# Eight banks of maxima on VectorE alone, and another order of steps, in a two-stream attention kernel

## The chip, the cores and the metric

The kernel runs on one core of one Trainium2 chip. The metric is the device time of one execution in microseconds; the number given for a kernel is the median of its runs.

## The reference

Two attention blocks A and B with the same input x (2048 tokens, 512 channels, 32 heads of 16) and weights of their own are mixed by a gate for each token. All arithmetic is in float32.

```python
def attention(x, wqkv, wo):                 # both blocks
    q, k, v = split(x @ wqkv)               # 32 heads of 16
    scores = einsum("bhqd,bhkd->bhqk", q, k) * 16 ** -0.5
    p = softmax(scores, axis=-1)
    o = einsum("bhqk,bhkd->bhqd", p, v)
    return merge_heads(o) @ wo

g = sigmoid((x * gate_w).sum(-1, keepdims=True))
out = g * attention(x, A_wqkv, A_wo) + (1 - g) * attention(x, B_wqkv, B_wo)
```

## The kernel before

The 64 heads of both blocks are worked through one after the other. A stage ahead of the main loop projects q, k and v, writes them to DRAM in high and low parts, and computes the maxima of the first head and of four more rounds. Then the main loop goes over `ROUNDS` = 64 x 16 *rounds*, two at a time; two rounds are called a *pair* here, and eight pairs make a head.

A round has three sorts of work.

- **Scores** (`score`, L594, letter `e`): the scores are computed transposed, keys on partitions. A round takes 128 keys and all 2048 queries: four products of 512 columns (L602), each into one of the three banks of `ps_st`, and ScalarE's exponential reads each (L604) into a quarter of `p`. `p` has three buffers, one per round. The row maximum is not subtracted by an engine: its two parts stand as two more rows in `q_st` (rows 48 and 49 of a half of 64 rows), against rows of -1 in `k_st`.
- **Maxima** (`max_product`, L116, letters `m`, `A`, `B`, `x`): the maxima are computed 20 rounds ahead of the scores that need them (`m = r + NT + LEAD`), with queries on partitions. A round takes 128 queries and all 2048 keys: four products of 512 columns (L128). The first two go into single banks (`ps_m1`, two buffers that alternate), the third and fourth (`A`, `B`) into the two banks of `ps_m2`, which has one buffer. VectorE reads a single bank, or both banks of `ps_m2` at once after `B`, and leaves a maximum for each query in `mxp` (L139).
- **V products** (`attend`, L555, digits): a round of `p` against V, for four stretches of keys in four column groups of TensorE (L563), accumulated over the 16 rounds of a head in the one bank `acc`. A digit says how many quarters of 128 queries follow; 4 is a whole round, 2 is half of one. Each `attend` writes eight matmul records into the trace. After the last round of a head ScalarE evicts `acc` (L580), and the next head's first V product waits for that.

Scores and maxima use 50 and 48 rows of TensorE's 128, so that two products, one on rows from 0 and one on rows from 64, run side by side; `rows()` alternates the halves, and each digit sets it back to 0.

The order of all of this is written out by hand as one string for a pair, and is the order in each engine's queue:

```python
    FULL = "eem4emeAeB2emex2AyeB"
    LATE = "ee2ee2ee2ee2"
```

`LATE` serves the last pairs, which have no maxima left to compute. With `x`, one single bank of the pair takes a detour (except in the one pair of a head whose second round is the head's last, `mm % NT == NT - 1`): ScalarE copies the bank to SBUF (L133), GpSimd takes the larger of the two halves in three steps (L134 to L136), and `y`, in the next pair, lets VectorE read the 256 maxima that remain (L147).

At special places of a head more is queued. At the end of the pair that completes a head's maxima VectorE makes `mrow` from `mxp` (L157) and GpSimd splits it (L158, L159). In the pair after, at a digit that comes after the third `e`, `max_rows` lets VectorE transpose it (`mt`, L164), and SP sends it out and back into `q_st` (L167, L169). Functions in `later` run ahead of a pair's first step: loads, the reciprocals of the denominators (`invert_den`, L400, twice after every eighth head), and others. Output projections (`project_out`, L436) run ahead of a pair's first digit; eight of the 64 heads have them, one in each of four pairs.

Of the kernel before, what the change touches and what calls it, by code (L numbers as in the profile page):

```python
# [23 lines left out]
F32 = mybir.dt.float32  # L24
# [3 lines left out]
ALU = mybir.AluOpType  # L28
AX = mybir.AxisListType
# [3 lines left out]
P = 128  # L33
# [4 lines left out]
NT = S // P  # L38
# [13 lines left out]
def gated_mha(ctx: ExitStack, tc: tile.TileContext, xT, x, wqkv_a, wo_a, wqkv_b, wo_b, gate_w, out):  # L52
    nc = tc.nc
    pe, act, dve, pool = nc.tensor, nc.scalar, nc.vector, nc.gpsimd
# [4 lines left out]
    small = ctx.enter_context(tc.tile_pool(name="small", bufs=2))  # L59
# [26 lines left out]
    def load_stacks(h, halves=HALVES):  # L86
        dma = nc.sync.dma_start
        s, hh = divmod(h, H)
        g, j = divmod(hh, HG)
        q, k = q_st[h % 3], k_st[h % 3]  # L90
        qs, ks = qd[s][g], kd[s][g]

        def pairs(t, step):
            v = t[0, j]
            return bass.AP(tensor=v.tensor, offset=v.offset, ap=[[S, DH], [step, 2], [1, S]])

        for b in halves:
            dma(k[b:b + 32].bitcast(F32), pairs(ks, HG * DH * S))
            dma(q[b:b + 32].bitcast(F32), pairs(qs, 0))
            dma(k[b + 32:b + 48].bitcast(F32), ks[0, j])  # L100
            dma(q[b + 32:b + 48].bitcast(F32), qs[1, j])
# [5 lines left out]
    PARTS = ((0,), (1,), (2, 3))  # L107
    mxp = {}
    turn = [0]
    banks_m, halved = {}, []  # L110

    def rows():
        turn[0] ^= 1
        return HALVES[1 - turn[0]]

    def max_product(m, c, fold=False):  # L116
        h, t = divmod(m, NT)
        if t == 0 and c == 0:
            mxp[h] = small.tile([P, NT, 3], F32, name="mxp")
        q, k = q_st[h % 3], k_st[h % 3]  # L120
        part = min(c, 2)
        if c < 3:
            n = len(PARTS[part])
            banks_m[m] = (ps_m1 if n == 1 else ps_m2).tile([P, n * 512], F32, name=f"ps_m{n}")
        ps = banks_m[m]
        b = rows()
        o = max(0, c - 2) * 512
        pe.matmul(ps[:, o:o + 512], q[b:b + SC, t * P:(t + 1) * P], k[b:b + SC, c * 512:(c + 1) * 512],  # L128
                  start=True, stop=True)
        if fold:  # L130
            x = small.tile([P, 512], F32, name="fold", bufs=2)
            d = x[:, :256]
            act.copy(x, ps)  # L133
            pool.tensor_tensor(d, d, x[:, 256:], op=ALU.subtract)  # L134
            pool.tensor_scalar(d, d, 3.4028234e38, 0.0, op0=ALU.min, op1=ALU.max)  # L135
            pool.tensor_tensor(d, d, x[:, 256:], op=ALU.add)  # L136
            halved.append((mxp[h][:, t, part:part + 1], d))
        elif c != 2:
            dve.tensor_reduce(mxp[h][:, t, part:part + 1], ps, op=ALU.max, axis=AX.X)  # L139

    def max_part(m, part):
        for c in PARTS[part]:
            max_product(m, c)

    def max_halved():
        o, d = halved.pop(0)
        dve.tensor_reduce(o, d, op=ALU.max, axis=AX.X)  # L147

    mparts = {}

    def max_split(h):
        halves = mxp.pop(h)
        m = small.tile([P, NT], F32, name="mrow")
        mp = small.tile([P, 2, NT], F32R, name="mparts")
        dve.tensor_reduce(m, halves, op=ALU.max, axis=AX.X)  # L157
        pool.tensor_copy(mp[:, 0], m)  # L158
        pool.tensor_tensor(mp[:, 1], m, mp[:, 0].bitcast(F32), op=ALU.subtract)  # L159
        mparts[h] = mp  # L160

    def max_rows(h):
        mt = small.tile([P, 32], F32, name="mt")
        dve.transpose(mt, mparts.pop(h).rearrange("p i t -> p (i t)").bitcast(F32))  # L164
        q = q_st[h % 3]
        r = md[h % 3]
        nc.sync.dma_start(r.rearrange("i (t a x) -> a (i t) x", a=4, x=32), mt)  # L167
        for b in HALVES:
            nc.sync.dma_start(q[b + SC:b + SC + 2].bitcast(F32), r)  # L169
# [266 lines left out]
    def project_out(side, t):  # L436
        groups = SIDES[side]
        ps = result_bank()
        c, tt = divmod(t, 4)
        sl = slice(tt * P, (tt + 1) * P)  # L440
        for G in groups:
            n, g = gh[G] * DH, G % NG
            slot = c if G == LAST else g
            for i, (a, b) in enumerate(((0, 0), (1, 0), (0, 1))):
                pe.matmul(ps, ot[a][:n, slot, sl], wt[b][:n, g], start=G == groups[0] and i == 0,  # L445
                          stop=G == groups[-1] and i == 2)
        g = gate[min(side, 1)][:, t:t + 1]
        if side == 0:
            dve.tensor_scalar(o_acc[:, t], ps, g, None, op0=ALU.mult)
        else:  # L450
            dve.scalar_tensor_tensor(o_acc[:, t], ps, g, o_acc[:, t], op0=ALU.mult, op1=ALU.add)
# [134 lines left out]
    def attend_next(n):  # L586
        while n:
            r, qa = divmod(done[0], 4)
            qb = min(4, qa + n)
            attend(r, qa, qb)  # L590
            done[0] += qb - qa
            n -= qb - qa

    def score(r, c):  # L594
        h, kt = divmod(r, NT)
        if c == 0:
            pt[r] = ppool.tile([P, S], F32, name="p")
        q, k = q_st[h % 3], k_st[h % 3]
        kk, cc = (4 * (kt % 4) + c, kt // 4) if h == NH - 1 else (kt, c)
        b = rows()  # L600
        ps = ps_st.tile([P, 512], F32, name="ps_st")
        pe.matmul(ps, k[b:b + SC + 2, kk * P:(kk + 1) * P], q[b:b + SC + 2, cc * 512:(cc + 1) * 512],  # L602
                  start=True, stop=True)
        act.activation(pt[r][:, c * 512:(c + 1) * 512], ps, AF.Exp, scale=SCALE)  # L604
# [1 line left out]

    FULL = "eem4emeAeB2emex2AyeB"
    LATE = "ee2ee2ee2ee2"  # L610
    after = {}

    for r in range(0, ROUNDS, 2):
        h, kt = divmod(r, NT)
        projects = []
        for rr in (r, r + 1):
            for fn, a in later.pop(rr, ()):
                if fn is project_out:
                    projects.append(a)
                else:  # L620
                    fn(*a)
        if kt == 0 and h + 2 < NH:
            load_stacks(h + 2)
        m = r + NT + LEAD
        scored = parts = 0
        waiting = len(halved)
        for step in FULL if m < ROUNDS else LATE:
            if step == "e":
                score(r + scored // 4, scored % 4)
                scored += 1  # L630
            elif step in "mABx":
                mm, c = m + parts // 4, parts % 4
                max_product(mm, c, step == "x" and mm % NT != NT - 1)
                parts += 1
            elif step == "y":
                if waiting:
                    max_halved()
            else:
                for a in projects:
                    project_out(*a)  # L640
                projects = []
                turn[0] = 0
                if r:
                    attend_next(int(step))
                if scored > 2 and r in after:
                    max_rows(after.pop(r))
        m += 1
        if m < ROUNDS and m % NT == NT - 1:
            max_split(m // NT)
            after[r + 2] = m // NT  # L650
# [29 lines left out]
```

## Time and profile before

| | |
|---|---|
| runs | 2844.14, 2844.75, 2844.58 us; median 2844.58 |
| profiled execution | span 2843.0 us; its own time outside the span is not listed, the runs' median is 1.6 us longer |
| TensorE clock granted | 0.998 |
| busy, of the span | TensorE 98%, VectorE 87%, ScalarE 85%, GpSimd 37% |
| chain that ended last | TensorE 74%, VectorE 16%, ScalarE 8%, issue 2% |
| main loop | from about 300 us to the end |

In rows of the profile PE is TensorE, PEld its weight loads, DVE VectorE, ACT ScalarE, POOL GpSimd, SP the engine that issues DMAs. A row of the timeline gives the start in us, the duration in us, engine, line, operation, output and inputs, and how many like instructions in a row are merged (x5); shapes are those of the first of them, and a bracket tells how long the engine had stood idle and who ended that. Records of one engine overlap a little, so that the distance from one start to the next is shorter than a duration. A row of busy times by stretch gives the stretch, its length, and for each engine busy us and instructions, then clock, DMA share and GB/s. A row of groups gives count, busy us, mean ns of one, idle time before and who ended it. A row of waits gives the total us, the number of waits and the longest.

### The profile page before, as it was taken

What the parts mean: (1) busy time and instruction counts of PE and PEld (TensorE: products, weight loads), DVE (VectorE), ACT (ScalarE), POOL (GpSimd) and SP (SyncE); (2) the same over time, 40 slices, a digit from 0 to 9 for tenths busy, and PEclk for the clock granted to TensorE, in tenths of its full rate; (3) what the DMA queues carried; (4) which work ended last, traced back from release to release, by engine and by line L of the source; (5) the groups of instructions that cost most, each with busy time, mean ns of one, the idle gap of its engine ahead of it and who ended that gap; (6) DMA issues with size and microseconds to landing.
All of it is one profiled execution on the core that took longest, in us unless ns stands there. A gap on an engine that the chain in (4) does not pass through costs nothing.

```text
span 2843.0 us, 56787 instructions
## 1 busy us (share of the span) xinstructions
PE 2795.6 (98%) x22168; PEld 1230.1 (43%) x22168; DVE 2464.7 (87%) x3367; ACT 2412.5 (85%) x4696; POOL 1042.4 (37%) x1686
## 2 busy tenths in 40 slices
PE   8999999999999999999999999999999999999999
PEld 6877433333333333333333444433333333334445
DVE  3135899999999999999999988899999999998884
ACT  3221799999999999999999877899999999998785
POOL 1000355453433333333433555333333344345431
PEclk9999999999999999999999999999999999999999
DMA  6673333222332222232432342232222233233302
GB/s 237 203 229 122 82 69 78 58 52 54 66 58 55 55 43 58 52 56 54 85 54 52 92 94 62 54 56 51 60 43 56 54 70 70 54 72 80 76 6 91
DMA packets 83747, 214.30 MB, mean 75 GB/s; under 512 B 21878, under 2 KB 32086, under 8 KB 70934
## 3 DMA queue, kind: packets, MB, share of 16 engines
q1 hardware_dynamic: 80918, 201.76, 31.2%
q0 software_dynamic: 2560, 8.91, 1.3%
q8 instruction: 174, 2.85, 0.4%
q14 instruction: 95, 0.78, 0.1%
HBM read 145.87 MB, written 64.74 MB: 74 GB/s over the span
## 4 chain that ended last, share of the span: by engine, by line
PE 74%; DVE 16%; ACT 8%; issue 2%; DMA 0%; SPq 0%; ACTq 0%
PE acc L563 28%; PE ps_st L602 22%; DVE mxp L139 14%; PE ps_m L128 12%; PE ps_pro L228 6%; ACT p L604 5%; PE ps_m L445 3%; PE ps_pro L251 3%; ACT ev L580 1%; ACT fold L133 1%; DVE mxp L147 1%; DMA raw<-in_xT 0%; DVE mrow L157 0%; PE ps_st L445 0%; DVE rn L400 0%
## 5 line engine op out<-in xcount | busy, mean ns | idle before, releaser
L139 DVE TENSOR_REDUCE mxp<-ps_m 128x1 f32<-128x512 f32 (+1 forms) x2633 | 2190.3, 890 | 135.1 <-PE ps_m L128 61.0
L604 ACT ACTIVATE p<-ps_st 128x512 f32<-128x512 f32 x4096 | 2153.5, 610 | 177.0 <-PE ps_m L128 100.5
L128 PE MATMUL ps_m<-k_st,q_st 48*128 48x512 f32 x4096 | 1407.2, 441 | 5.3 <-DVE mxp L139 0.8
L602 PE MATMUL ps_st<-q_st,k_st 50*128 50x512 f32 x4096 | 1379.8, 438 | 0.0
L563 PE MATMUL acc<-p,vg 128*17 128x256 f32 (+1 forms) x12360 | 1182.8, 455 | 29.5 <-ACT ev L580 28.0
L602 PEld LDWEIGHTS ps_st<-q_st,k_st 50*128 50x128 f32 x4096 | 662.1, 184 | 801.6 <-ACT p L604 748.0
L128 PEld LDWEIGHTS ps_m<-k_st,q_st 48*128 48x128 f32 x4096 | 677.1, 184 | 251.8 <-DVE mxp L139 233.0
L134 POOL TENSOR_TENSOR fold<-fold 128x256 f32<-128x256 f32 x439 | 321.1, 731 | 1096.5 <-ACT fold L133 1096.5
L563 PEld LDWEIGHTS acc<-p,vg 128*17 128x17 f32 x12360 | 205.3, 95 | 466.3 <-issue 414.6
L136 POOL TENSOR_TENSOR fold<-fold 128x256 f32<-128x256 f32 x439 | 322.1, 734 | 36.6
L133 ACT COPY fold<-ps_m 128x512 f32<-128x512 f32 x439 | 261.3, 595 | 0.0
L135 POOL TENSOR_SCALAR fold<-fold 128x256 f32<-128x256 f32 x439 | 175.6, 400 | 38.5
L147 DVE TENSOR_REDUCE mxp<-fold 128x1 f32<-128x256 f32 x439 | 179.5, 409 | 0.0
L158 POOL CAST mparts<-mrow 128x16 fp32r<-128x16 f32 x64 | 12.6, 197 | 401.0 <-DVE mrow L157 401.0
L232 ACT CAST part<-ps_pro 128x1024 fp32r<-128x1024 f32 x32 | 32.5, 1015 | 132.9 <-PE ps_pro L228 132.9
L233 DVE TENSOR_TENSOR part<-ps_pro,part 128x1024 fp32r<-128x1024 f32 x32 | 39.2, 1225 | 111.4 <-ACT part L232 111.4
L445 PE MATMUL ps_m<-wo,ot 128*128 128x512 f32 (+1 forms) x354 | 90.9, 401 | 0.0
L254 ACT COPY v_st<-ps_pro 128x512 f32<-128x512 f32 x31 | 18.2, 587 | 77.4 <-PE ps_pro L251 77.4
L228 PE MATMUL ps_pro<-xh,whi 128*128 128x512 f32 x256 | 73.0, 404 | 8.8 <-ACT xh L214 8.7
L180 POOL DMA_DIRECT2D vg<-vd x32 | 25.6, 799 | 137.5 <-DMA vd<-v_st 137.1
L445 PEld LDWEIGHTS ps_m<-wo,ot 128*128 128x128 f32 (+1 forms) x354 | 63.9, 188 | 21.3 <-ACT fold L133 7.0
L228 PE MATMUL ps_pro<-xh,wlo 128*128 128x512 f32 x256 | 69.7, 395 | 0.0
(94 smaller groups left out, 822.1 us busy)
## 6 DMA issues: line engine op xcount, KB each, us to landing
k_st<-kd SPq DMA_DIRECT2D x128, 256.0 KB
q_st<-qd SPq DMA_DIRECT2D x128, 256.0 KB
qd<-part SPq DMA_DIRECT2D x32, 512.0 KB
kd<-part SPq DMA_DIRECT2D x32, 512.0 KB
k_st<-kd SPq DMA_DIRECT2D x128, 128.0 KB
q_st<-qd SPq DMA_DIRECT2D x128, 128.0 KB
od<-ev SPq DMA_DIRECT2D x63, 256.0 KB
vd<-v_st SPq DMA_DIRECT2D x32, 272.0 KB
```

Of the source, the lines that this page charges most:

```text
L128: pe.matmul(ps[:, o:o + 512], q[b:b + SC, t * P:(t + 1) * P], k[b:b + SC, c * 512:(c + 1) * 512], start=True, stop=True)
L133: act.copy(x, ps)
L134: pool.tensor_tensor(d, d, x[:, 256:], op=ALU.subtract)
L135: pool.tensor_scalar(d, d, 3.4028234e38, 0.0, op0=ALU.min, op1=ALU.max)
L136: pool.tensor_tensor(d, d, x[:, 256:], op=ALU.add)
L139: dve.tensor_reduce(mxp[h][:, t, part:part + 1], ps, op=ALU.max, axis=AX.X)
L147: dve.tensor_reduce(o, d, op=ALU.max, axis=AX.X)
L228: pe.matmul(ps[:, c * 512:(c + 1) * 512], a[:, k], b[:, k], start=n == 0, stop=n == 3 * KC - 1)
L445: pe.matmul(ps, ot[a][:n, slot, sl], wt[b][:n, g], start=G == groups[0] and i == 0, stop=G == groups[-1] and i == 2)
L563: pe.matmul(acc[32 * c:32 * c + 17, qa * P:qb * P], v[:, 4 * a + c if final else kt, j], p[:, c * 512 + qa * P:c * 512 + qb * P], start=fi ...
L602: pe.matmul(ps, k[b:b + SC + 2, kk * P:(kk + 1) * P], q[b:b + SC + 2, cc * 512:(cc + 1) * 512], start=True, stop=True)
L604: act.activation(pt[r][:, c * 512:(c + 1) * 512], ps, AF.Exp, scale=SCALE)
```

## The change

`FULL` becomes `"e2emem2ABmeee4emeAB"`. The letters `x` and `y` go, and with them ScalarE's copy, GpSimd's three steps and VectorE's read of the halved tile: the sixth product of a pair becomes an ordinary `m`, whose bank VectorE reads whole. The V products come in bursts of 2, 2 and 4 in place of 4, 2 and 2. `LATE`, the stage ahead of the loop and everything else stay.

```diff
-    banks_m, halved = {}, []
+    banks_m = {}
...
-    def max_product(m, c, fold=False):
+    def max_product(m, c):
...
-        if fold:
-            x = small.tile([P, 512], F32, name="fold", bufs=2)
-            d = x[:, :256]
-            act.copy(x, ps)
-            pool.tensor_tensor(d, d, x[:, 256:], op=ALU.subtract)
-            pool.tensor_scalar(d, d, 3.4028234e38, 0.0, op0=ALU.min, op1=ALU.max)
-            pool.tensor_tensor(d, d, x[:, 256:], op=ALU.add)
-            halved.append((mxp[h][:, t, part:part + 1], d))
-        elif c != 2:
+        if c != 2:
             dve.tensor_reduce(mxp[h][:, t, part:part + 1], ps, op=ALU.max, axis=AX.X)
...
-    def max_halved():
-        o, d = halved.pop(0)
-        dve.tensor_reduce(o, d, op=ALU.max, axis=AX.X)
...
-    FULL = "eem4emeAeB2emex2AyeB"
+    FULL = "e2emem2ABmeee4emeAB"
...
-            elif step in "mABx":
-                mm, c = m + parts // 4, parts % 4
-                max_product(mm, c, step == "x" and mm % NT != NT - 1)
+            elif step in "mAB":
+                max_product(m + parts // 4, parts % 4)
                 parts += 1
-            elif step == "y":
-                if waiting:
-                    max_halved()
```

More of the change, by code (lines that the diff above doesn't have):

```diff
@@ L625, in gated_mha @@
         scored = parts = 0
-        waiting = len(halved)
         for step in FULL if m < ROUNDS else LATE:
```

## The prediction

> **What bounds the kernel now.** Two rounds make a *pair*: eight products for maxima (four banks read singly, four in twos), eight products for scores with their exponentials on ScalarE, and V products in three bursts. 502 pairs follow one another; eight pairs make a head. I first read busy time in two stretches: an ordinary one, and one in which output projections (L445) run as well.
>
> ```profile
> 1000.00:1050.00 50.00, 49.50 (x430) 19.09 (x426) 48.20 (x66) 48.47 (x96) 18.62 (x32) 1.00 0.21 39
> 1600.00:1650.00 50.00, 49.54 (x374) 23.09 (x372) 40.11 (x55) 37.01 (x74) 26.51 (x37) 1.00 0.40 92
> ```
>
> After the 50.00 come TensorE, weight loads, VectorE, ScalarE, GpSimd. TensorE is full in both, but its busy time is modelled. VectorE (48.20) and ScalarE (48.47) have under 2 us of 50 to spare in the first stretch and 10 and 13 in the second. So I look at who comes last inside a pair. The timeline of VectorE alone:
>
> ```profile
> 1003.97 4.15 DVE L139 TENSOR_REDUCE mxp<-ps_m 128x1 f32<-128x1024 f32 x5
> 1008.04 0.41 DVE L147 TENSOR_REDUCE mxp<-fold 128x1 f32<-128x256 f32 x1
> 1008.59 4.75 DVE L139 TENSOR_REDUCE mxp<-ps_m 128x1 f32<-128x1024 f32 x6
> 1013.25 0.41 DVE L147 TENSOR_REDUCE mxp<-fold 128x1 f32<-128x256 f32 x1
> 1013.58 1.22 DVE L139 TENSOR_REDUCE mxp<-ps_m 128x1 f32<-128x1024 f32 x1
> 1014.83 0.20 DVE L157 TENSOR_REDUCE mrow<-mxp 128x16 f32<-128x48 f32 x1
> 1014.95 0.68 DVE L139 TENSOR_REDUCE mxp<-ps_m 128x1 f32<-128x512 f32 x1
> ```
>
> The first row is a pair in which one bank goes by ScalarE and GpSimd: five reads, 4.07 us from start to the next start, then the read of the halved tile (L147), then 1008.59: a pair of 4.62. After 1008.04 the short read needs 0.33 (1013.25 to 1013.58), but 0.55 pass: VectorE idles 0.22 of that pair. The third row is the one pair of a head without that detour (`mm % NT == NT - 1`): all eight banks, six reads, with nothing idle between, **4.66** from 1008.59 to 1013.25. So one read of a bank adds 4.66 - 4.07 = 0.59, and one of two banks 1.15. TensorE in the pair before:
>
> ```profile
> 1004.10 1.05 PE L563 MATMUL acc<-p,vg 128*17 128x512 f32 x8
> 1005.08 0.49 PE L602 MATMUL ps_st<-q_st,k_st 50*128 50x512 f32 x1
> ...
> 1006.04 0.62 PE L563 MATMUL acc<-p,vg 128*17 128x256 f32 x8
> 1006.60 0.49 PE L602 MATMUL ps_st<-q_st,k_st 50*128 50x512 f32 x1
> ...
> 1007.27 0.63 PE L563 MATMUL acc<-p,vg 128*17 128x256 f32 x8
> ...
> 1008.73 1.05 PE L563 MATMUL acc<-p,vg 128*17 128x512 f32 x8
> ```
>
> A pair takes TensorE 1008.73 - 1004.10 = 4.63, and VectorE waits for it. So an ordinary pair is TensorE's today, by a hair, and the change makes every pair like the third row above.
>
> **What a head takes now.** The eviction of `acc` (L580) comes once a head:
>
> ```profile
> 989.61 0.62 ACT L580 COPY ev<-acc 128x512 f32<-128x512 f32 x1
> ```
> ```profile
> 1027.57 0.62 ACT L580 COPY ev<-acc 128x512 f32<-128x512 f32 x1
> ...
> 1028.24 1.05 PE L563 MATMUL acc<-p,vg 128*17 128x512 f32 x8 [0.45 <-ACT ev L580]
> ```
> ```profile
> PE acc L563 <- ACT ev L580: 28.0, 62, 0.5
> ```
>
> One head is 1027.57 - 989.61 = 37.96. Eight pairs at 4.62 would be 36.96; the other 1.00 is the pair without detour, the row maxima and the eviction, for which TensorE stands 0.45 (28.0 us in 62 waits over the run).
>
> **The change, part by part.** *VectorE.* Eight pairs of 4.66 are 37.28. `mrow` (L157) waits for the read before it: 1013.58 to 1014.95 is 1.37 in place of 1.15, +0.22. The transpose `mt` (L164) adds 0.12:
>
> ```profile
> 1017.28 0.20 DVE L164 STREAM_TRANSPOSE mt<-mparts 128x32 f32<-128x32 f32 x1
> 1017.40 0.65 DVE L139 TENSOR_REDUCE mxp<-ps_m 128x1 f32<-128x512 f32 x1
> ```
>
> VectorE's floor for a head is thus 37.62, 0.34 under today's 37.96: what the detour saves in most pairs, each head gives back at its three special places. (By the mean durations of the records, 680 and 1219 ns, a pair would be 4 x 0.680 + 2 x 1.219 = 5.16; the records overlap, and I go by starts.)
>
> ```profile
> L139 DVE TENSOR_REDUCE mxp<-ps_m 128x1 f32<-128x1024 f32 x1024 | 1248.4, 1219 | 64.7 <-PE ps_st L602 19.8 <-PE ps_m L128 5.2
> L139 DVE TENSOR_REDUCE mxp<-ps_m 128x1 f32<-128x512 f32 x1609 | 1057.9, 680 | 70.4 <-PE ps_m L128 55.8 <-PE ps_st L602 11.0
> ```
>
> *TensorE.* Old runs of products between bursts: six (after the burst of 4), four, six. New: four between the bursts of 2, six, then six after the burst of 4. The bursts, runs and partners (rows 0 and 64 side by side) are as many as before, so TensorE alone needs 4.63 again, hidden under 4.66. New are pairs of A with B and of two scores. Two maxima products side by side do occur in the projections before the main loop, four products in 0.73, as fast as mixed ones, so I add nothing:
>
> ```profile
> 289.29 0.73 PE L128 MATMUL ps_m<-k_st,q_st 48*128 48x512 f32 x4
> ```
>
> *Can TensorE feed VectorE without a gap?* VectorE's order is m1, m2, AB1, m3, m4, AB2; single banks alternate between two buffers. The tightest ring: m1 read, so its buffer is free; m3 is written there (the second partners of "ABmeee"), then "ee", the burst of 4, and m4 with the next run's first products; VectorE reads m4 and AB2, and is at m1 again. Prices, from a place where a product waited for VectorE:
>
> ```profile
> 1014.85 0.18 PEld L128 LDWEIGHTS ps_m<-k_st,q_st 48*128 48x128 f32 x1
> ```
> ```profile
> 1014.48 0.50 PE L602 MATMUL ps_st<-q_st,k_st 50*128 50x512 f32 x1
> ...
> 1014.85 0.49 PE L128 MATMUL ps_m<-k_st,q_st 48*128 48x512 f32 x1
> ...
> 1015.18 0.39 PE L128 MATMUL ps_m<-k_st,q_st 48*128 48x512 f32 x1
> 1015.51 0.41 PE L563 MATMUL acc<-p,vg 128*17 128x256 f32 x4
> ```
> ```profile
> 1013.00 1.57 ACT L604 ACTIVATE p<-ps_st 128x512 f32<-128x512 f32 x3 [0.16 <-PE ps_st L602]
> 1015.02 0.60 ACT L604 ACTIVATE p<-ps_st 128x512 f32<-128x512 f32 x1 [0.44 <-PE ps_st L602]
> ```
>
> The read of 1013.58 ends at 14.80, the weights load at 14.85 (0.05), the next products follow 0.33 later, V again 0.33 later. The burst of 4 takes 0.98 to the next product (1004.10 to 1005.08), a run's first product 0.50, its reader starts 0.04 after (14.98 to 15.02). Ring: 0.68 + 0.05 + 0.33 + 0.33 + 0.98 + 0.50 + 0.04 + 0.59 + 1.15 = **4.65**. Under 4.66, by 0.01: VectorE stays the bound, but with no margin.
>
> *ScalarE* loses the copy, 0.59 a pair; GpSimd loses all three halving steps, for which only L147 waited. ScalarE now has eight exponentials at (1.57 - 0.60) / 2 = 0.48, 3.9 of 4.66. With three banks for scores, the sixth exponential frees the bank of the ninth product; reckoned as below it ends at 2.83, that product could go on at 2.98 (0.05, and 0.10 since its load is late: 0.49 against 0.39), and would by itself at about 2.93: a hold of 0.05, of the size that the run of 1005.08 has in its 0.96 now, so inside TensorE's 4.63.
>
> *Eviction.* Today it queues behind exponentials and the copy, and the burst of 4 waits. Afterwards a head ends with the burst of 4. With m1's read at 0: m3 and a score start at 0.73, the exponentials of "eee" at 1.27 (0.73 + 0.54), 1.75 and 2.23, the burst of 4 at 1.39, the eviction at 2.72 to 3.34, so the burst of 2 starts at 3.39 (0.05 as at 1028.24); by itself it would at 1.39 + 0.98 + 0.96 = 3.33. That is 0.06. But the next two exponentials slip by 0.28, the second ends at 4.28, the score that takes its bank loads at 4.33, the second burst of 2 starts at 4.76 (0.33 + 0.10), the run "ABmeee" at 5.32 (0.56 as 1006.04 to 1006.60), and m3 at 5.65, where VectorE would have allowed 4.66 + 0.73 + 0.10 = 5.49. VectorE waits **0.16** at m4. Bounds: 0, if the run ahead covers it, and today's 0.45.
>
> A head: 37.28 + 0.22 + 0.12 + 0.16 = 37.78, 0.18 less than now.
>
> *Other moves.* `max_rows`, with one DMA out and two back on SP, goes to the second burst, which is earlier; its score is three pairs off, no cost. `project_out` goes ahead of a burst of 2; in its heads VectorE has 10 of 50 us idle, so I take 0 for these eight heads (0.18 gained in each at best, 1.4 us; 0.06 lost in 32 pairs, 1.9, at worst). The reciprocals (L400) stand between reads:
>
> ```profile
> L400 DVE RECIPROCAL rn<-dn 128x64 f32<-128x64 f32 x14 | 7.6, 543 | 0.0
> ```
>
> 0.543 each, less 0.08 by which records overlap (the short read: 0.41 in 0.33), is 0.46, 6.4 in all. Today seven heads pay for two each; from the eviction before such a head to that at its end:
>
> ```profile
> 913.11 0.61 ACT L580 COPY ev<-acc 128x512 f32<-128x512 f32 x1
> ```
> ```profile
> 951.64 0.62 ACT L580 COPY ev<-acc 128x512 f32<-128x512 f32 x1
> ```
>
> 38.53 - 37.96 = 0.57 a head, 4.0 in all: +2.4 net.
>
> **Sum.** 63 evictions less 8 heads with projections: 55 x -0.18 = -9.9, +2.4, 0: **-7.5 us**. The profiled execution's span is 2843.0, and 1.6 us lie around it to the median of 2844.58; 2835.5 and 2837.1. A measurement of this kernel can tell about 0.2%, 5.7 us, from no change.
>
> **A rule against it.** The Trainium skill, "TensorEngine Tiling (Array Packing)", section "PSUM Bottleneck", advises to use ScalarE and VectorE both for emptying PSUM, since tiled products outrun it. The change takes a bank away from ScalarE. By that rule the change costs, as (b) below. The trace agrees that VectorE is the next bound; that a head's floor on VectorE, 37.62, lies under today's 37.96 speaks against it.
>
> **The rivals.** *(a) The ring takes over, slower.* 0.01 is the whole margin, and each further 0.01 costs 0.01 x 8 x 55 = 4.4 us; from 4.68 on the gain is gone. If one more weight load isn't hidden (0.49 - 0.39 = 0.10 between a run's first and later products), the ring is 4.75, the head 38.50: +0.54 x 55 + 2.4 = 32 us, 2877. For it: m3 would wait for VectorE in every pair, in mid-run, as the product of 1014.85 did. Against it: that delay is in my 0.33. *(b) A head keeps its special price of 1.00*, of which only 0.34 is VectorE's own: 37.28 + 1.00 = 38.28, +0.32 x 55 + 2.4 = +20, 2865. For it: 62 waits of TensorE for the eviction now; against it: the copy ahead of it is gone. *(c) The eviction is hidden whole:* 37.62, -0.34 x 55 + 2.4 = -16.3, 2828. *(d) Reads follow one another at the full 5.16:* +0.50 x 8 x 55 - 7.5 = +212, 3057. The Trainium skill, "VectorE: DVE Perf Modes", section "Terms", says that an operation can't issue until the pipe of the one before is empty; the third row of VectorE's timeline, 4.66 for six, speaks against (d).
>
> **How the numbers follow.** Forecast 0.45, (a) 0.30, (b) 0.12, (c) 0.12, (d) 0.01. The forecast's own range is 2832 to 2843 (0.1 a head either way): of its 0.45, 0.30 lie under 2838.9, 0.14 within 0.2%, 0.01 above. (a) spreads from 2838 to 2877: 0.02 within, 0.28 above. (b) and (d) are slower, (c) faster. Faster 0.42, same 0.16, slower 0.42. The range for 8 in 10 reaches from (c) to two thirds into (a): 2828 to 2866; the upper part of (a) and (d) are left out.
>
> **What would show it.** Right: VectorE's timeline as one row of reads from `mrow` to `mt` and on, 4.66 a pair, busy near 50 of 50; waits of VectorE for products only after an eviction, some 0.16; evictions 37.78 apart; TensorE's waits for ScalarE at L563 far under 28 us. Wrong: waits of VectorE for L128 in every pair, above all at m4 (the ring); a pair over 4.68; TensorE waiting as long as now at the head's end.

## The result, and the profile after

| | before | after |
|---|---|---|
| median | 2844.14 us (2843.87 to 2844.75, 5 runs) | **2854.41 us** (2854.15 to 2854.99, 5 runs) |
| span of the profiled execution | 2843.0 us | 2852.4 us |
| ratio | | 1.0036 [1.0023, 1.0049] |

The kernel is slower by 10.3 us, where 7.5 us less was forecast. The time lies inside the range, in the part that belongs to rival (a). Lines have moved: of the names in the prediction, L139 is now L131, L563 L549, L602 L588, L604 L590, L580 L566, L157 L143, L164 L150, L445 L431 (in the two runs with a short read, one line further down).

Two lines of the page after, busy time and the chain that ended last:

```profile
PE 2829.6 (99%) x22168; PEld 1295.9 (45%) x22168; DVE 2559.5 (90%) x3367; ACT 2242.5 (79%) x4257; POOL 225.6 (8%) x369
...
PE 88%; DVE 9%; ACT 1%; DMA 1%; issue 0%; SPq 0%; ACTq 0%
```

ScalarE and GpSimd lost what they should lose (85% to 79%, 37% to 8%). Of the chain that ended last, ScalarE's 8% fell to 1% and VectorE's 16% to 9%, and TensorE's 74% rose to 88%: a first sign against "VectorE is the bound". Busy time by stretch, the two stretches of the prediction:

```profile
1000.00:1050.00 50.00, 49.95 (x426) 20.39 (x418) 49.87 (x66) 44.74 (x87) 0.42 (x2) 1.00 0.21 39
1600.00:1650.00 50.00, 50.00 (x372) 24.66 (x368) 42.17 (x55) 34.31 (x67) 11.37 (x13) 1.00 0.45 91
```

VectorE shows 49.87 of 50, as predicted. The timeline of VectorE is the unbroken row that was to prove the forecast right, without one bracket in a whole head:

```profile
1436.04 0.20 DVE L143 TENSOR_REDUCE mrow<-mxp 128x16 f32<-128x48 f32 x1
1436.16 1.28 DVE L131 TENSOR_REDUCE mxp<-ps_m 128x1 f32<-128x512 f32 x2
1437.36 0.20 DVE L150 STREAM_TRANSPOSE mt<-mparts 128x32 f32<-128x32 f32 x1
1437.48 36.51 DVE L131 TENSOR_REDUCE mxp<-ps_m 128x1 f32<-128x1024 f32 x46
1474.03 0.20 DVE L143 TENSOR_REDUCE mrow<-mxp 128x16 f32<-128x48 f32 x1
```

But the head takes 1474.03 - 1436.04 = 37.99, not 37.78: no idle time is shown, and yet 0.21 is lost. The answer is in the single reads, one pair of VectorE's timeline, read by read (AB2, m1, m2, AB1, m3, m4, AB2):

```profile
997.06 1.21 DVE L131 TENSOR_REDUCE mxp<-ps_m 128x1 f32<-128x1024 f32 x1
998.19 0.68 DVE L131 TENSOR_REDUCE mxp<-ps_m 128x1 f32<-128x512 f32 x1
998.79 0.68 DVE L131 TENSOR_REDUCE mxp<-ps_m 128x1 f32<-128x512 f32 x1
999.39 1.21 DVE L131 TENSOR_REDUCE mxp<-ps_m 128x1 f32<-128x1024 f32 x1
1000.52 0.68 DVE L131 TENSOR_REDUCE mxp<-ps_m 128x1 f32<-128x512 f32 x1
1001.15 0.69 DVE L131 TENSOR_REDUCE mxp<-ps_m 128x1 f32<-128x512 f32 x1
1001.75 1.21 DVE L131 TENSOR_REDUCE mxp<-ps_m 128x1 f32<-128x1024 f32 x1
```

From start to start a single read takes 0.60 and a double one 1.13: 4 x 0.60 + 2 x 1.13 = 4.66, the floor of the prediction. One step is longer: m3 to m4, 1000.52 to 1001.15, takes **0.63**. VectorE waits 0.03 for m4, in every ordinary pair, and the pair is 1001.75 - 997.06 = 4.69. The views show no idle time there, because a read is recorded for 0.68 and the next can start after 0.60: a wait of up to 0.08 only makes the overlap of two records smaller. The Trainium skill, "Perfetto Trace Analysis", section "Optimizing Scalar/DVE Operations", says that the fixed overhead of an operation shows about twice as long in a profile as it keeps the engine busy, since its write-acknowledgement half overlaps with the next instruction. The trace agrees: 512 columns more cost 0.53 in both counts (1.21 - 0.68, 1.13 - 0.60), which leaves, as an estimate, a fixed 0.15 in the record and 0.07 from start to start.

TensorE's side of the same pair: the weight load (PEld) of m3, the two scores behind it ("ee"), the burst of 4, and the next two products, the second of which is m4.

```profile
998.93 0.18 PEld L128 LDWEIGHTS ps_m<-k_st,q_st 48*128 48x128 f32 x1
...
999.27 0.40 PE L588 MATMUL ps_st<-q_st,k_st 50*128 50x512 f32 x2
999.60 1.05 PE L549 MATMUL acc<-p,vg 128*17 128x512 f32 x8
1000.58 0.50 PE L588 MATMUL ps_st<-q_st,k_st 50*128 50x512 f32 x1
1000.58 0.50 PE L128 MATMUL ps_m<-k_st,q_st 48*128 48x512 f32 x1
```

The ring of the prediction, term by term (forecast in brackets): m1's read 0.68 (0.68), to m3's weight load 998.93 - 998.87 = 0.06 (0.05), to "ee" 0.34 (0.33), to the burst of 4 0.33 (0.33), to the next products 0.98 (0.98), m4's product 0.50 (0.50), to its reader 1001.15 - 1001.08 = **0.07** (0.04), to AB2 0.60 (0.59), to m1 1.13 (1.15). The sum is 4.69, against 4.65 forecast and VectorE's 4.66. By this account the ring is the bound; the first two experiments test it.

### The profile page after: what moved, and what is told of

Same layout as the page of the kernel before. It is cut to its first block, busy times and chain, and to the rows that moved or that the text cites. A ratio compares the mean times of both kernels' runs of the same rounds, so it can differ in the third digit from the quotient of the medians.

```text
span 2852.4 us, 54552 instructions
## 1 busy us (share of the span) xinstructions
PE 2829.6 (99%) x22168; PEld 1295.9 (45%) x22168; DVE 2559.5 (90%) x3367; ACT 2242.5 (79%) x4257; POOL 225.6 (8%) x369
## 4 chain that ended last, share of the span: by engine, by line
PE 88%; DVE 9%; ACT 1%; DMA 1%; issue 0%; SPq 0%; ACTq 0%
PE acc L549 34%; PE ps_st L588 26%; PE ps_m L128 16%; DVE mxp L131 8%; PE ps_pro L214 6%; PE ps_m L431 3%; PE ps_pro L237 3%; ACT p L590 1%; DMA k_st<-kd 1%; DMA raw<-in_xT 0%; PE ps_st L431 0%; DVE rn L386 0%; ACT ev L566 0%; PE ps_st L482 0%; PE ps_m L482 0%
## 5 line engine op out<-in xcount | busy, mean ns | idle before, releaser
L131 DVE TENSOR_REDUCE mxp<-ps_m 128x1 f32<-128x512 f32 (+1 forms) x3072 | 2423.0, 858 | 41.1 <-PE ps_m L128 30.7
L590 ACT ACTIVATE p<-ps_st 128x512 f32<-128x512 f32 x4096 | 2146.2, 601 | 357.8 <-PE ps_st L588 222.9
L128 PE MATMUL ps_m<-k_st,q_st 48*128 48x512 f32 x4096 | 1290.5, 455 | 8.4 <-DVE mxp L131 6.5
L588 PE MATMUL ps_st<-q_st,k_st 50*128 50x512 f32 x4096 | 1272.8, 439 | 0.4 <-ACT p L590 0.3
L549 PE MATMUL acc<-p,vg 128*17 128x256 f32 (+1 forms) x12360 | 1183.6, 455 | 1.9 <-ACT ev L557 1.4
L588 PEld LDWEIGHTS ps_st<-q_st,k_st 50*128 50x128 f32 x4096 | 593.2, 184 | 687.7 <-ACT p L590 650.0
L128 PEld LDWEIGHTS ps_m<-k_st,q_st 48*128 48x128 f32 x4096 | 596.0, 184 | 312.5 <-DVE mxp L131 211.8
L549 PEld LDWEIGHTS acc<-p,vg 128*17 128x17 f32 x12360 | 205.3, 95 | 465.3 <-issue 443.4
L431 PE MATMUL ps_m<-wo,ot 128*128 128x512 f32 (+1 forms) x354 | 90.8, 401 | 0.0
L431 PEld LDWEIGHTS ps_m<-wo,ot 128*128 128x128 f32 (+1 forms) x354 | 64.0, 188 | 20.2 <-issue 7.8
L214 PE MATMUL ps_pro<-xl,whi 128*128 128x512 f32 x256 | 69.2, 393 | 0.0
L214 PEld LDWEIGHTS ps_pro<-xh,whi 128*128 128x128 f32 x256 | 48.0, 191 | 22.8 <-ACT xh L200 9.7
L214 PEld LDWEIGHTS ps_pro<-xh,wlo 128*128 128x128 f32 x256 | 48.6, 190 | 10.3
L214 PEld LDWEIGHTS ps_pro<-xl,whi 128*128 128x128 f32 x256 | 48.6, 190 | 10.2
L404 POOL TENSOR_TENSOR o_num<-o_num,rb 128x512 f32<-128x512 f32 x28 | 35.5, 1283 | 103.9 <-DMA rb<-rd 103.9
```

The lines of the kernel that those rows point to most:

```text
L214: pe.matmul(ps[:, c * 512:(c + 1) * 512], a[:, k], b[:, k], start=n == 0, stop=n == 3 * KC - 1)
L404: (dve if G == LAST else pool).tensor_tensor(num[:n], num[:n], rb[:n], op=ALU.mult)
L549: pe.matmul(acc[32 * c:32 * c + 17, qa * P:qb * P], v[:, 4 * a + c if final else kt, j], p[:, c * 512 + qa * P:c * 512 + qb * P], start=fi ...
```

## The experiments

The first four ran beside runs of the kernel before with a median of 2844.52 us, the others beside 2845.02.

### The maxima product first of its pair

```diff
-    FULL = "e2emem2ABmeee4emeAB"
+    FULL = "e2emem2ABmeee4meeAB"
```

> The new order with the fourth single bank's product ahead of its partner score ("4meeAB" for "4emeAB"), nothing else. Ring theory (the pair of 4.69 us is the way from the read of m1, by m3, "ee", the burst of 4 and m4, to the read of AB2 and back to m1): m4's reader starts 0.07 after the product's end because its partner's semaphore goes ahead; as the first of the two it should start 0.04 after, so the pair falls by 0.03 to 4.66, 0.03 x 470 = 14 us, to about 2840. TensorE theory (the new order itself needs 4.69 of TensorE): no change, 2854. VectorE theory (eight banks with their gaps are 4.69): no change, 2854.

Measured: 2843.08 us (2841.16 to 2844.87), ratio to before 0.9994 [0.9985, 1.0003]: 11.3 us less than the changed kernel by the medians, by an exchange of two letters that adds and removes no work (about 2840 was expected; the pair at the eviction, 4.90, and the one behind `mt`, 4.75, gained nothing). VectorE's timeline, read by read (AB1, m3, m4, AB2, and AB1 of the next pair), and the products after the burst of 4:

```profile
997.22 1.22 DVE L131 TENSOR_REDUCE mxp<-ps_m 128x1 f32<-128x1024 f32 x1
998.35 0.68 DVE L131 TENSOR_REDUCE mxp<-ps_m 128x1 f32<-128x512 f32 x1
998.95 0.69 DVE L131 TENSOR_REDUCE mxp<-ps_m 128x1 f32<-128x512 f32 x1
999.55 1.22 DVE L131 TENSOR_REDUCE mxp<-ps_m 128x1 f32<-128x1024 f32 x1
...
1001.88 1.22 DVE L131 TENSOR_REDUCE mxp<-ps_m 128x1 f32<-128x1024 f32 x1
```
```profile
998.40 0.50 PE L128 MATMUL ps_m<-k_st,q_st 48*128 48x512 f32 x1
998.41 0.73 PE L588 MATMUL ps_st<-q_st,k_st 50*128 50x512 f32 x2
```

m4's product ends at 998.90 and its reader starts at 998.95, 0.05 after and not 0.07; m3 to m4 is 0.60 again, the pair 1001.88 - 997.22 = 4.66, the ordinary head 37.82. What follows: the ring was the bound, and VectorE's 4.66 a pair was right. The two products side by side start and end together in the records, and the reader of the second in the order starts 0.02 to 0.03 later. A rule of the Trainium skill fits that, "TensorE: Matmul & The Clock Gate", section "The cost: per-tile semaphore tail": the semaphore increments of products that end together go one after another, at 26.3 ns each. The trace agrees in size; the rows do not show the increments themselves. The first product always stands on the rows from 0 and the second on those from 64, so this exchange alone can't tell the order from the rows; the next experiment has a row that can.

### A short read of m2, and a short read of m4

```diff
-            dve.tensor_reduce(mxp[h][:, t, part:part + 1], ps, op=ALU.max, axis=AX.X)
+            v = ps[:, :64] if c == 1 and t % 2 == 0 else ps
+            dve.tensor_reduce(mxp[h][:, t, part:part + 1], v, op=ALU.max, axis=AX.X)
```

This is for m2, which is no part of the ring; for m4, which is part of it and of VectorE's sum alike, the condition is `t % 2 == 1`.

> The new order, but of the bank m2 (second bank of the first round of a pair) VectorE reads 64 of 512 columns; the maxima then are of fewer keys. VectorE's own sum falls from 4.66 to about 4.2 a pair, and m2's read does not lie on the ring. Ring theory: the pair stays at 4.69, 2850 to 2854, with VectorE idle 0.47 a pair. VectorE theory: the pair falls to TensorE's 4.6, about 2815. TensorE theory: 4.69, as the ring.

> As the run before, but 64 columns of m4 (second bank of the second round), whose read lies on the ring. Ring theory: the ring falls to about 4.2, VectorE to 4.2, the pair to TensorE's own 4.60 to 4.63, 2805 to 2825. VectorE theory: the same. TensorE theory: 4.69 stays, 2850 to 2854. Only with the run before it tells the ring from the sum.

Measured: with the short m2 2852.02 us (ratio 1.0024 [1.0015, 1.0034]), with the short m4 2818.51 (0.9910 [0.9896, 0.9923]). VectorE's timeline with the short m2, then its waits from 1000 to 1500, then the timeline with the short m4:

```profile
996.60 2.55 DVE L132 TENSOR_REDUCE mxp<-ps_m 128x1 f32<-128x512 f32 x4
999.31 1.82 DVE L132 TENSOR_REDUCE mxp<-ps_m 128x1 f32<-128x1024 f32 x2 [0.15 <-PE ps_m L128]
1001.29 2.55 DVE L132 TENSOR_REDUCE mxp<-ps_m 128x1 f32<-128x512 f32 x4 [0.16 <-PE ps_m L128]
```
```profile
DVE mxp L132 <- PE ps_m L128: 24.9, 117, 0.4
```
```profile
997.54 4.43 DVE L132 TENSOR_REDUCE mxp<-ps_m 128x1 f32<-128x1024 f32 x6 [0.20 <-PE ps_m L128]
1002.18 1.23 DVE L132 TENSOR_REDUCE mxp<-ps_m 128x1 f32<-128x1024 f32 x1 [0.21 <-PE ps_m L128]
```

With the short m2 a pair is still 1001.29 - 996.60 = 4.69: VectorE got time to spare, stands idle in every pair for products, and the kernel gains next to nothing. Nor can VectorE's own sum be the bound, then. Time taken out of the ring counts: with the short m4 a pair is 1002.18 - 997.54 = 4.64 at this place and 4.62 as a rule, which is the 4.63 that the prediction gives TensorE by itself.

The run with the short m2 also tells the order of two products from their rows. A and B of the first round stand side by side, B second and on the rows from 64, but no engine waits for A alone:

```profile
998.76 0.51 PE L128 MATMUL ps_m<-k_st,q_st 48*128 48x512 f32 x2
```

They end at 999.27, and VectorE, idle before, starts at 999.31: 0.04 after, as behind a first product. So the 0.07 belongs neither to the rows nor to being second as such; it is seen where the partner has a reader of its own to signal, which fits the rule above.

### The order of before, without the detour

```diff
-    FULL = "e2emem2ABmeee4emeAB"
+    FULL = "eem4emeAeB2emem2AeB"
```

> The order of before, with the detour taken out: "eem4emeAeB2emem2AeB", VectorE reads all eight banks. Ring theory: no burst of 4 lies between the products that reuse m1's bank and the next, VectorE's own 4.66 a pair is left, a head near 37.6 to 37.8, 2828 to 2840, faster than before and after. If eight banks on VectorE are themselves what costs (VectorE theory), 2854 or more, with waits at the end of a head as before. TensorE theory: 4.66 a pair, 2840.

Measured: 2831.07 us (2830.54 to 2831.56), ratio 0.9953 [0.9940, 0.9965]. Two evictions on ScalarE, a head apart:

```profile
947.30 0.59 ACT L566 COPY ev<-acc 128x512 f32<-128x512 f32 x1
...
984.86 0.59 ACT L566 COPY ev<-acc 128x512 f32<-128x512 f32 x1
```

The head is 37.56, 0.06 under the 37.62 that was forecast as VectorE's floor, which was thus a little too high. A few heads are longer, up to 40.63, and bring the mean of the 45 ordinary ones to 37.70; in four of them a score waits for the DMA of the row maxima, 3.7 us in all. Its pairs are 4.66, and the pair at the head's boundary is 4.67, so that the eviction costs nothing. To take the detour away is thus worth 13.5 us by itself. The other half of the change, the order, takes 23 us back.

### The new order, with the detour kept

```diff
-    FULL = "eem4emeAeB2emex2AyeB"
+    FULL = "e2emem2ABymeee4exeAB"
```

> The kernel before with the new order of steps alone, the detour kept for the same bank (the second single bank of the second round, now after the burst of 4): "e2emem2ABymeee4exeAB". ScalarE's copy then stands between two exponentials whose banks the next two runs of products need; they free 0.47 later, TensorE waits. Expected 4.9 to 5.1 a pair, 2960 to 3040: the new order can't carry the detour at this place. If the ring alone limited it (the bank m4 off the ring, since ScalarE reads it), 4.62 a pair and 2830.

Measured: 3007.59 us, ratio 1.0569 [1.0550, 1.0588]. Of the timeline, two bursts of 4, ScalarE's copy, and the first and third product of the run between the bursts of 2, the third with its weight load:

```profile
1000.49 1.05 PE L563 MATMUL acc<-p,vg 128*17 128x512 f32 x8
...
1002.50 0.58 ACT L133 COPY fold<-ps_m 128x512 f32<-128x512 f32 x1
...
1003.00 0.50 PE L602 MATMUL ps_st<-q_st,k_st 50*128 50x512 f32 x1
...
1003.63 0.18 PEld L602 LDWEIGHTS ps_st<-q_st,k_st 50*128 50x128 f32 x1 [0.45 <-ACT p L604]
1003.63 0.50 PE L602 MATMUL ps_st<-q_st,k_st 50*128 50x512 f32 x1
...
1005.53 1.05 PE L563 MATMUL acc<-p,vg 128*17 128x512 f32 x8
```

A pair is 5.04. The score of 1003.63 comes 0.63 after its run's first in place of 0.33: the copy stands between exponentials on ScalarE, and the weight load waits for an exponential to free its bank. The halves of the change cannot be added up: the new order does not carry the detour at this bank. Another bank was not tried in it.

### The detour at another bank

This is before's code in another order. The bank of the detour now belongs to the first round of a pair, so the one pair of a head without detour is named by `mm % NT == NT - 2`. First m1, then m2:

```diff
-    FULL = "eem4emeAeB2emex2AyeB"
+    FULL = "ex4yemeeAB2emem2eAeB"
```
```diff
-    FULL = "eem4emeAeB2emex2AyeB"
+    FULL = "2emex2AyBeeem4meAeBe"
```

> The detour by ScalarE and GpSimd is kept, but for the first bank of a pair, in an order laid out so that no ring and no wait for score banks exceeds TensorE's own sum: "ex4yemeeAB2emem2eAeB" (no detour in the pair with mm % NT == NT - 2). Ring theory, with its prices (a product's reader 0.04 or 0.07 after its end, a freed bank 0.05 to the weights load): VectorE's floor is 4.4 a pair, TensorE's 4.55, nothing else above; a head near 37.2 to 37.4, 2800 to 2815, faster than all others. If what limits is a sum of all three engines near 4.6 that no order can lower, 2830 to 2845.

> As the run before, with the detour for the second bank and other places: "2emex2AyBeeem4meAeBe". Here the ring from m1 by m3 to m4 stays, without m2's read and with m4 the first of its two products: 4.65, so the ordinary pair falls no further than 4.60 to 4.66 and a head to 37.4 or more, 2815 to 2830. If the ring is a wrong account, about as the run before.

Measured: 2816.04 us with m1 (2815.27 to 2816.23, ratio 0.9896 [0.9881, 0.9911]), just above what was expected, and 2827.91 with m2 (0.9938 [0.9925, 0.9950]), within it, but not by the ring of 4.65 that was given for it: its ordinary pairs are 4.62 too, and the pair with `mrow` is 5.01, the one at the eviction 4.87. The first is the fastest version found, 29 us under before and 38 under after. Two of its evictions:

```profile
939.42 0.64 ACT L580 COPY ev<-acc 128x512 f32<-128x512 f32 x1
...
976.81 0.65 ACT L580 COPY ev<-acc 128x512 f32<-128x512 f32 x1
```

With m1 a head is 37.39, less than VectorE's floor for eight banks. Its ordinary pairs are 4.62, as before, and not the 4.55 that was expected of TensorE; what holds them was not tried. What it saves is at the head's special places. The pairs before were 5.15 at the eviction, 4.77 without the detour and 5.03 with `mrow`; here the pair at the eviction is 4.67, the one after it and the one without the detour are 4.85, and the one with `mrow` is 4.55. The loss that the change went after was in the place of the detour, more than in the detour.

### Projections only ahead of the burst of 4

```diff
-                for a in projects:
-                    project_out(*a)
-                projects = []
+                if step == "4" or m >= ROUNDS:
+                    for a in projects:
+                        project_out(*a)
+                    projects = []
```

> The changed kernel, with project_out ahead of the burst of 4 again, as before, in place of the first burst of 2. Account from the trace: VectorE's read of a projection takes 0.75, the burst of 2 that follows 0.56, so the second single bank of the next run waits for its buffer, 0.13 in each of 32 pairs; a burst of 4 covers the read. Expected 3 to 4 us less than the changed kernel: 2850.5 to 2851.5. If the 0.13 comes from elsewhere (the ring), no change, 2854.4.

Measured: 2853.51 us (2852.72 to 2854.19), ratio 1.0029 [1.0019, 1.0040], which overlaps the changed kernel's own; 0.9 us less by the medians, where 3 to 4 were expected. The account behind it was of this stretch of TensorE's timeline, in the changed kernel: a projection, the burst of 2 that follows it, the run of four products, the next burst.

```profile
1620.75 2.99 PE L431 MATMUL ps_m<-wo,ot 128*128 128x512 f32 x12
1623.67 0.63 PE L549 MATMUL acc<-p,vg 128*17 128x256 f32 x8
1624.23 0.49 PE L588 MATMUL ps_st<-q_st,k_st 50*128 50x512 f32 x1
...
1624.58 0.49 PE L128 MATMUL ps_m<-k_st,q_st 48*128 48x512 f32 x1
1625.01 0.63 PE L549 MATMUL acc<-p,vg 128*17 128x256 f32 x8
```
```profile
1623.78 0.75 DVE L435 TENSOR_SCALAR o_acc<-ps_m,gate 128x512 f32<-128x512 f32 x1 [1.61 <-PE ps_m L431]
```

VectorE's read of the projection ends at 24.53, and m2's product of 24.58 starts right behind it: this short run takes 0.78 (1624.23 to 1625.01), 0.67 elsewhere. With projections ahead of the burst of 4 three of four projection pairs are indeed 0.06 shorter, but the one with `mrow` is 0.19 longer, so that the four together gain nothing; what is gained, 0.2 a head, lies in the pair at the eviction that ends such a head (4.69 in place of 4.90 in all eight). The delay behind the projection is real, then, but to move the projection only moves it. The pair with `mrow` is now 0.24 over its neighbours, the price of `mrow` in an ordinary pair; why it cost nothing there before stays open.

## Why the prediction was wrong

The step that failed is "Under 4.66, by 0.01: VectorE stays the bound", and with it the forecast; what happened is rival (a), at 0.04 beyond the forecast ring.

- **The ring's sum.** "its reader starts 0.04 after" was taken from a score that stood first of its pair. m4 stands second, where it is 0.07. With 0.01 each at the freed buffer, the next run and m4's read, and 0.02 less at AB2, 4.65 becomes 4.69. Every other term held. The rival's own guess of the cause, one more weight load of 0.10 that isn't hidden, was wrong: "that delay is in my 0.33" held (0.34).
- **VectorE's floor**, 4.66 a pair: right, shown by the exchange of two letters, which leaves just that. Rival (d), 5.16, is out.
- **TensorE alone**, 4.63: it held as the time of a pair in which VectorE has time to spare (4.62 with the short m4). Single pairs are shorter (4.56 in the kernel before), so not all of it is TensorE's own work.
- **Row maxima and transpose.** `mrow` costs 0.23 (0.22 forecast), `mt` 0.05 (0.12). With the short m2, which gives VectorE time to spare, the pair behind `mt` is 4.69 and `mt` costs nothing, while `mrow` costs as much as here: part of `mt` falls into time in which VectorE waits anyway.
- **The eviction.** 0.20 was measured at that pair (4.895 against 4.69), 0.16 forecast, by the mechanism that was given. Eviction on ScalarE, then bursts and runs on TensorE:

```profile
1029.40 0.60 ACT L566 COPY ev<-acc 128x512 f32<-128x512 f32 x1
```
```profile
1028.04 1.05 PE L549 MATMUL acc<-p,vg 128*17 128x512 f32 x8
1029.03 0.50 PE L588 MATMUL ps_st<-q_st,k_st 50*128 50x512 f32 x1
...
1030.05 0.63 PE L549 MATMUL acc<-p,vg 128*17 128x256 f32 x8
1030.61 0.50 PE L588 MATMUL ps_st<-q_st,k_st 50*128 50x512 f32 x1
...
1031.04 0.50 PE L588 MATMUL ps_st<-q_st,k_st 50*128 50x512 f32 x1
...
1032.94 1.05 PE L549 MATMUL acc<-p,vg 128*17 128x512 f32 x8
```

  The eviction ends at 1030.00 and the burst of 2 starts 0.05 behind it, 1.02 after its run in place of 0.97; then the second product pair starts 0.43 after the first in place of 0.33, since its score's bank comes free late, and the pair is 1032.94 - 1028.04 = 4.90. So TensorE still waits for the eviction, once a head and by about 0.05, as forecast. The list of waits shows 0.5 us over the run, where 28.0 stood; the wait can be seen at the burst's weight load, and in the distance from start to start:

```profile
PE acc L549 <- ACT ev L566: 0.5, 1, 0.5
```
```profile
1030.05 0.13 PEld L549 LDWEIGHTS acc<-p,vg 128*17 128x17 f32 x8 [0.30 <-ACT ev L566]
```

  So rival (b), the special price of 1.00, did not hold, and (c), no price at all, is what the old order without the detour has.
- **A head**, so: 8 x 4.69 + 0.20 + 0.23 + 0.05 = 38.00, where 37.78 was forecast and 37.96 measured before.
- **Reciprocals**: the seven heads that hold them cost 0.80 over an ordinary one, 0.57 before: 7 x 0.23 = 1.6 net, forecast 2.4.
- **Projections**: "I take 0" failed. Each of the eight heads is 0.44 longer, 3.5 us, above the worst case that was given (1.9). VectorE's 10 idle us of 50 hide nothing where a product has to wait for one read of it; in the trace the short run behind a projection is 0.11 longer in all four pairs of such a head that hold one. Three of the four are 0.13 to 0.14 longer than before, and the one with `mrow` is about as long as before.

Of the 17 us between forecast and result, the ring's 8 x 0.03 in each of 55 heads is 13, and the projections are 3.5; smaller terms of both signs make up the rest. The difference of the spans, after less before, is 9.4 us. From the distances between evictions: 45 ordinary heads +3.5 (1.1 of it in the last one, whose eviction falls among the pairs without maxima), seven with reciprocals +2.0, eight with projections +3.5, the head in which the gate is computed +0.35 and the one after it -0.2, up to the first eviction +0.35.

The advice in the Trainium skill's "TensorEngine Tiling (Array Packing)", section "PSUM Bottleneck", to let ScalarE and VectorE both empty PSUM, was set aside in the prediction by the floor of 37.62. The floor was nearly right, and the advice is borne out all the same: the fastest version keeps a bank on ScalarE, and its head of 37.39 is under that floor.

## What to carry to other kernels

Where a chain through buffers comes within a few hundredths of an engine's own sum, don't ask which of them is longer: a margin of 0.01 us on nine terms decides nothing, and an order that gives the chain slack is the safer edit. Look for a short wait in the distance from start to start of like instructions, not in idle time. Of two products side by side, put the one whose reader is waited for first, or beside one that no engine waits for; and before an operation is moved to another engine to remove a stall, try it at another place in the order.

## What the runs showed of the hardware

- The reader of the second of two products that run side by side started 0.07 us after the modelled end, that of the first 0.04 to 0.05; behind a second product whose partner no engine waits for it was 0.04. Repeated in every ordinary pair, this and the ring behind it are 11 us here.
- VectorE can wait in every ordinary pair of some 500 while its timeline shows no gap: a read of 512 columns is recorded as 0.68 us, the next can start after 0.60, and a wait of 0.03 shows only as a start 0.63 after the last.
